# Attention rounds with one weight split each, the next q and k split first, and the sixth sigmoid behind the decoding

## The chip, the cores and the metric

The kernel runs on one core of a Trainium2 chip. Its engines work side by side, each through its own instructions in their order: TensorE (PE, with its weight loads as PEld), VectorE (DVE), ScalarE (ACT), GpSimd (POOL) and SyncE (SP), whose queue issues nearly all DMAs. The metric is the device time of one execution in microseconds (us); of several executions the median counts.

## The reference

Two parts follow each other. The first is an attention with a sigmoid in place of the softmax, for 8 batches, 12 heads, 448 positions and a head size of 64:

```python
scores = scale * np.matmul(q, k.transpose(0, 1, 3, 2)) - np.log(S)
attn = 1.0 / (1.0 + np.exp(-scores))
out = np.matmul(attn, v)
```

The second takes the heads of a position together as x (3584 x 768) and computes a maxout layer with weights of 768 x 768:

```python
h = np.maximum(np.maximum(x @ w1, x @ w2), x @ w3)
return h @ w_out
```

q, k and v come as float32, the weights as 64-bit floats, which the kernel receives as pairs of integers.

## The kernel before, in words

**Precision by splitting.** Most matrix products are made from three products of parts: a tensor is cast to a reduced format (hi) and the remainder is kept (lo), and hi·hi, hi·lo and lo·hi are summed. A split is therefore a cast and a subtraction. For q and k `qk_split` makes it on VectorE (lines 321 and 322, on 128x896 elements); for the weights `w_split` makes it (lines 156 and 157, on 128x384), in the attention on VectorE too.

**The attention in rounds.** `attention` runs 24 rounds (`for n in range(count)`, n from 0 to 23). A round handles four heads, as two pairs; each pair's q and k lie in one tile of 448 KB (`load_qk`, line 302). The 448 keys are three chunks of 128 and one of 64. In a round TensorE does, in this order:

- the scores of the round's second pair, chunks 0 to 2 (line 330, 18 matmuls), read out by `shared_scores`: VectorE copies one head's half (line 385), ScalarE takes the sigmoid of the other (line 387);
- the scores of the next round's first pair, chunks 0 to 2 (line 330, 18 more), each read out by one sigmoid on ScalarE over both heads (line 312). These are called first scores here;
- the products with v (line 350, 24 matmuls);
- the scores of the short fourth chunk for the next round (line 342) and their sigmoid (line 312), and the product of the present round's fourth chunk (line 359).

The score tiles have three buffers in PSUM (`ps_s`), taken in turn. So the first scores of chunk 0 reuse the tile of the second pair's chunk 0, and wait until line 385 and line 387 have read it.

Between the three large sigmoids of the first scores ScalarE also takes the sigmoid of the halves that VectorE copied (`raw_sigmoid`, line 396): large, half, large, half, large, half. The sixth sigmoid of the change's title is the third large one, which goes behind the decoding.

**Work laid beside the rounds.** In each round VectorE and ScalarE also decode one block of the weights (`decode`): ScalarE by lines 178 and 179, VectorE by lines 180, 184, 188 and 189, where line 188 needs line 179. There are three weights q, and for each eight blocks: four that are used first (rounds 0 to 3, 8 to 11, 16 to 19), after the second to fourth of which GpSimd forms sums of blocks (line 144), and four that go back to DRAM (rounds 4 to 7, 12 to 15, 20 to 23) by a DMA that SyncE issues at line 207 and that waits for line 189. Each weight gives seven splits. Before the change `split_weights` makes up to two a round as soon as a weight's four blocks are decoded: rounds 4 to 7, 12 to 15 and 20 to 23 hold 2, 2, 2 and 1. From round 9 on, a slice of the attention's own output is loaded again in each round (line 221, 224 KB), for twelve rounds, and GpSimd forms differences of such slices (line 232).

**The orders.** All of it is pinned in program order on each engine. VectorE's order in a round is: copy out a result of the round before (line 377), three copies of line 385, line 377 again, the split of the next round's second pair, the weight splits, the decoding, and the split of the first pair of the round after that (lines 321 and 322 again). SyncE's order is: load v of the next round (line 307), load the two q and k tiles of the round after that (line 302, twice), store two results (line 378), load a raw weight block (line 168), store the decoded block (line 207, in the rounds named above), load the slice (line 221, in twelve rounds).

The buffers of hi and lo are two of each, so the split of the later first pair overwrites what the present round's first scores read.

After the rounds come four stages of matrix products (line 469), on the same tiles; the first of them needs the splits of x (lines 263 and 267).

Of the kernel before, what the change touches and what calls it, by code (L numbers as in the profile page):

```python
# [27 lines left out]
PRODUCTS = (  # L28
    ("a11", "b11", 0),
    ("s2", "t2", 1),  # L30
    ("s3", "t3", 3),
    ("s1", "t1", 2),
    ("a12", "b21", 0),
    ("a22", "t4", 1),
    ("s4", "b22", 2),
)
# [3 lines left out]
def attention_then_maxout(  # L40
# [35 lines left out]
    C = S // P  # L76
# [50 lines left out]
    def w_stage():  # L127
        return {name: ws_p.tile([P, HP], F32, name=f"ws_{name}") for name in BLOCKS}

    W_ORDER = (("a21", ()), ("a22", ("s1",)), ("a11", ("s2", "s3")), ("a12", ("s4",)))
    W_SUMS = {
        "s1": ("a21", "a22", ALU.add),
        "s2": ("s1", "a11", ALU.subtract),
# [4 lines left out]
    def w_combine(r, names):  # L140
        for name in names:
            r[name] = r["a21"] if name == "s3" else ws_p.tile([P, HP], F32, name=f"ws_{name}")
            in0, in1, op = W_SUMS[name]
            pin(nc.gpsimd.tensor_tensor(out=r[name], in0=r[in0], in1=r[in1], op=op))  # L144

    def w_load(st, q):
        r = w_stage()
        for name, sums in W_ORDER:
            pin(nc.sync.dma_start(out=r[name], in_=w_dram[st, q][:, BLOCKS.index(name)]))
        for name, sums in W_ORDER:  # L150
            w_combine(r, sums)
        return r

    def w_split(q, name, r, copy):
        hi, lo = w_tiles(q, name)
        pin(copy(out=hi, in_=r[name]))
        pin(nc.vector.tensor_tensor(out=lo, in0=r[name], in1=hi.bitcast(F32), op=ALU.subtract))

    def decoding(dec_p, todo, bufs, ahead, square_p):
# [11 lines left out]
        def decode(raw, out):  # L171

            words = raw.bitcast(U32).rearrange("p a (c two) -> p (a c) two", two=2)
            low, high = words[:, :, 0], words[:, :, 1]
            square = square_p.tile([P, S], F32, name="c")[:, :HP]
            bits = dec_p.tile([P, HP], U32, name="wb", bufs=bufs)
            out = bits.bitcast(F32) if out is None else out
            pin(nc.scalar.activation(out=square, in_=high.bitcast(F32), func=AF.Square))  # L178
            pin(nc.scalar.activation(out=low, in_=low, func=AF.Copy, scale=2.0**-29))
            pin(nc.vector.tensor_scalar(  # L180
                out=bits, in0=high, scalar1=3, scalar2=0x3FFFFFF8,
                op0=ALU.logical_shift_left, op1=ALU.bitwise_and,
            ))
            pin(nc.vector.scalar_tensor_tensor(
                out=bits, in0=high, scalar=0xC0000000, in1=bits,
                op0=ALU.bitwise_and, op1=ALU.bitwise_or,
            ))
            pin(nc.vector.tensor_tensor(out=bits, in0=bits, in1=low, op=ALU.add))
            pin(nc.vector.scalar_tensor_tensor(
                out=out, in0=square, scalar=LEAST**2, in1=bits.bitcast(F32),  # L190
                op0=ALU.is_ge, op1=ALU.mult,
            ))
            return out

        for k, (st, q, n) in enumerate(todo):
# [4 lines left out]
            if st == 0:  # L200
                if n == BLOCKS.index(W_ORDER[0][0]):
                    stage = w_stage()
                decode(raws[k], stage[BLOCKS[n]])
                w_combine(stage, dict(W_ORDER)[BLOCKS[n]])
                yield q, stage
# [65 lines left out]
    def attention(stack):  # L271
# [12 lines left out]
        for q in range(3):  # L284
            todo += [(0, q, BLOCKS.index(name)) for name, _ in W_ORDER]
            todo += [(1, q, n) for n in range(4)]
        background = decoding(dec_p, todo, 2, 3, sq_p)
        splits = []

        def decode():  # L290
            done = next(background)
            if done:
                q, stage = done
                decoded.append(q)
                if decoded.count(q) == len(BLOCKS):
                    splits.extend((q, name, stage) for name, _, _ in PRODUCTS)

        decoded = []

# [5 lines left out]
        def load_v(b, f):  # L305
            t = v_p.tile([P, 14, D], F32, name="v")
            pin(nc.sync.dma_start(out=t, in_=v[b, f]))
            return t

        def sigmoid(ps):  # L310
            a = a_p.tile([P, 2, S], F32, name="a")
            pin(nc.scalar.activation(  # L312
                out=a, in_=ps[:, :, :S], func=AF.Sigmoid, bias=bias_s, scale=scale
            ))
            return a[:, 0], a[:, 1]

        def qk_split(t):

            hi = hl_p.tile([P, 2 * S], F32R, name="hi")
            lo = hl_p.tile([P, 2 * S], F32R, name="lo")  # L320
            pin(nc.vector.tensor_copy(out=hi, in_=t))
            pin(nc.vector.tensor_tensor(out=lo, in0=t, in1=hi.bitcast(F32), op=ALU.subtract))
            return (hi, hi), (hi, lo), (lo, hi)

        def scores(terms, c):
            ps = ps_s.tile([P, 2, 512], F32, name="ps_s")
            for n, (kt, qt) in enumerate(terms):
                for e in range(2):
                    r = slice(e * D, (e + 1) * D)
                    pin(nc.tensor.matmul(  # L330
                        ps[:, e, :S], kt[r, S + c * P : S + (c + 1) * P], qt[r, :S],
                        start=n == 0, stop=n == len(terms) - 1,
                    ))
            return ps
# [31 lines left out]
        def load(n):  # L366
            b, f = fours[n]
            return load_qk(b, 2 * f), load_qk(b, 2 * f + 1)

        def finish(n, pss, pool=m_p, names=("m11", "m12"), gs=range(2)):  # L370
            if n < 0:
                return
            b, f = fours[n]
            for g in gs:
                k = 2 * f + g
                o = pool.tile([P, S], F32, name=names[g])
                pin(nc.vector.tensor_copy(out=o, in_=pss[g][:, :S]))
                pin(nc.sync.dma_start(
                    out=x_dram[k // HALF][:, k % HALF, b * S : (b + 1) * S], in_=o
                ))  # L380
# [14 lines left out]
        def raw_sigmoid(a):  # L395
            pin(nc.scalar.activation(
                out=a[1], in_=a[1], func=AF.Sigmoid, bias=bias_s, scale=scale
            ))

        def split_weights():  # L400
            for _ in range(2):
                if splits:
                    w_split(*splits.pop(0), nc.vector.tensor_copy)

        xs, count, pss = {}, len(fours), None
# [6 lines left out]
        for n in range(count):  # L412
            ahead = n + 1 < count
            if ahead:
                next_vt = load_v(*fours[n + 1])
                later_ts = load(n + 2) if n + 2 < count else None
            if n == 0:
                first_terms = qk_split(next_ts[0])
            finish(n - 1, pss, gs=(0,))
            second = [shared_scores(scores(second_terms, c), c) for c in range(C)]  # L420
            finish(n - 1, pss, gs=(1,))
            if ahead:
                second_terms = qk_split(next_ts[1])
            next_first = []
            for c in range(C):
                if ahead:
                    next_first.append(sigmoid(scores(first_terms, c)))
                raw_sigmoid(second[c])
            split_weights()
            decode()  # L430
            if n + 2 < count:
                first_terms = qk_split(later_ts[0])

            part = n - 9
            if 0 <= part < 4 * HALF:
                k, block = divmod(part, 4)
                row, th = ((0, 1), (0, 0), (1, 1), (1, 0))[block]
                x_block(xs, x_dram, 0, row, th, k)
                x_combine(xs, ((), ("t1",), ("t2", "t3"), ("t4",))[block], (k,))
            if n == count - 1:  # L440
                t_store(xs, 0)
                for name in FIRST:
                    x_lo(*x_hi(name, xs))
            pss = [ps_av.tile([P, 512], F32, name=f"ps_av{g}") for g in range(2)]
            for g, weights in enumerate((first, second)):
                for c in range(C):
                    weigh(pss[g], vt, g, c, weights[c])
            next_last = sigmoid(last_scores(next_ts)) if ahead else None
            last_weigh(pss, vt, last)
            if ahead:  # L450
                vt, first, next_ts, last = next_vt, next_first, later_ts, next_last
# [3 lines left out]
    with ExitStack() as stack:  # L455
        xs, finish = attention(stack)
# [196 lines left out]
```

## Time and profile before

| | us |
|---|---|
| median of 3 runs | 873.5 (873.43 to 874.3) |
| the profiled execution, its own time | 874.69 |
| its span in the trace | 872.6 |
| TensorE busy | 858.6 |
| VectorE busy | 661.8 |
| ScalarE busy | 412.5 |
| GpSimd busy | 183.4 |

The profile is of one execution. The span is the time from the first to the last instruction in the trace; the rest of the profiled execution's own time, 2.1 us, lies around it. Busy times are sums over instructions without their waits. In a line of the timeline stand the start, the duration, the engine, the kernel's line, the operation, what it writes and reads, and, in brackets, the idle time of the engine before it and what ended it. A wait is listed as the waiting engine and line, then what it waited for, the total, the times and the longest. The granted TensorE clock is 1.00 throughout.

### The profile page before, as it was taken

The numbers are of one execution on the slowest core, as the hardware profiler recorded it, in microseconds if no ns is written. First come the engines' busy times: TensorE is split into PE (matmuls) and PEld (weight loads), VectorE is DVE, ScalarE is ACT, GpSimd is POOL, SyncE is SP. The second block draws the span as 40 slices with busy tenths as digits, with TensorE's granted clock in tenths as the row PEclk, the third lists the DMA queues.
The fourth block names the chain that finished last, engine by engine and source line by source line (L and its number), as shares of the span: only waits on it lengthen the run. The fifth ranks groups of instructions, "written<-read, shape, count | busy, mean of one in ns | idle before, by whom it ended". The sixth has DMA issues, their size and how long they took to land. (4 is left out here: it accounts for less than half of the span.)

```text
span 872.6 us, 13085 instructions
## 1 busy us (share of the span) xinstructions
PE 858.6 (98%) x4842; PEld 698.7 (80%) x4842; DVE 661.8 (76%) x947; ACT 412.5 (47%) x571; POOL 183.4 (21%) x148
## 2 busy tenths in 40 slices
PE   8999999999999999999999999999999999999998
PEld 4555555555549999999999999999999998999997
DVE  5789878997887868589596888969688798737452
ACT  6778877787783404242352434225344352413320
POOL 0100022012200762702100020210002463760600
PEclk9999999999999999999999999999999999999999
DMA  6667676776638465513836552484653416262422
GB/s 229 207 216 243 225 236 223 251 260 244 216 123 311 164 232 173 191 50 114 324 113 259 196 195 70 131 305 143 235 220 148 169 58 221 90 211 95 170 74 84
DMA packets 74479, 161.88 MB, mean 186 GB/s; under 512 B 6960, under 2 KB 53936, under 8 KB 74416
## 3 DMA queue, kind: packets, MB, share of 16 engines
q1 hardware_dynamic: 74272, 160.94, 52.4%
q8 instruction: 38, 0.62, 0.3%
q14 instruction: 25, 0.20, 0.1%
q10 hardware_dynamic: 144, 0.11, 0.0%
HBM read 109.90 MB, written 51.12 MB: 185 GB/s over the span
## 5 line engine op out<-in xcount | busy, mean ns | idle before, releaser
L469 PE MATMUL ps_y<-xhi_t,wlo_s 128*128 128x448 f32 x432 | 156.8, 363 | 0.0
L469 PE MATMUL ps_y<-xhi_t,whi_s 128*128 128x448 f32 x432 | 156.6, 362 | 0.0
L469 PE MATMUL ps_y<-xlo_t,whi_s 128*128 128x448 f32 x432 | 155.5, 360 | 0.0
L312 ACT ACTIVATE a<-ps_s,bias_s 128x896 f32<-128x896 f32 x96 | 96.5, 1005 | 46.6 <-PE ps_s L342 33.4
L469 PE MATMUL ps_y<-xhi_b,wlo_a 128*128 128x448 f32 x288 | 104.7, 363 | 0.0
L469 PE MATMUL ps_y<-xhi_b,whi_a 128*128 128x448 f32 x288 | 104.4, 362 | 0.0
L469 PE MATMUL ps_y<-xlo_b,whi_a 128*128 128x448 f32 x288 | 103.8, 360 | 0.2 <-DVE xlo_b L267 0.2
L579 ACT COPY p<-ps_y 128x448 f32<-128x448 f32 x48 | 25.5, 531 | 157.6 <-PE ps_y L469 157.5
L144 POOL TENSOR_TENSOR ws_s<-ws_a,ws_a 128x384 f32<-128x384 f32 x12 | 13.4, 1116 | 408.4 <-DMA ws_a<-w_dram 309.9
L469 PEld LDWEIGHTS ps_y<-xhi_t,whi_s 128*128 128x128 f32 x432 | 81.1, 188 | 6.5
L469 PEld LDWEIGHTS ps_y<-xlo_t,whi_s 128*128 128x128 f32 x432 | 80.8, 187 | 5.6
L469 PEld LDWEIGHTS ps_y<-xhi_t,wlo_s 128*128 128x128 f32 x432 | 81.1, 188 | 4.2
L553 DVE TENSOR_TENSOR m<-ps_y,u 128x448 f32<-128x448 f32 x71 | 43.8, 620 | 50.8 <-PE ps_y L469 49.3
L582 DVE TENSOR_TENSOR u<-ps_y,p 128x448 f32<-128x448 f32 x48 | 29.8, 622 | 53.9 <-PE ps_y L469 49.9
L232 POOL TENSOR_TENSOR xs_t<-xs_b,xs_t 128x448 f32<-128x448 f32 x48 | 63.1, 1341 | 36.0 <-DMA xs_b<-x_dram 35.8
L551 ACT COPY m<-ps_y 128x448 f32<-128x448 f32 x24 | 12.8, 533 | 121.0 <-PE ps_y L469 114.2
L267 DVE TENSOR_TENSOR xlo_t<-xs_t,xhi_t 128x1344 fp32r<-128x1344 f32 x42 | 67.8, 1614 | 0.0
L267 DVE TENSOR_TENSOR xlo_b<-xs_b,xhi_b 128x1344 fp32r<-128x1344 f32 x42 | 67.2, 1599 | 0.1
L330 PE MATMUL ps_s<-hi 64*128 64x448 f32 x282 | 57.8, 395 | 5.4 <-DVE half L385 5.2
L178 ACT ACTIVATE c<-wraw 128x384 f32<-128x384 f32 x48 | 26.7, 556 | 74.6 <-DVE m L559 43.6
L263 ACT CAST xhi_t<-xs_t 128x1344 fp32r<-128x1344 f32 x42 | 55.4, 1318 | 12.2 <-PE ps_y L469 8.0
L263 ACT CAST xhi_b<-xs_b 128x1344 fp32r<-128x1344 f32 x42 | 55.4, 1318 | 9.6 <-PE ps_y L469 9.6
(71 smaller groups left out, 1820.5 us busy)
## 6 DMA issues: line engine op xcount, KB each, us to landing
qk<-qk SPq DMA_DIRECT2D x48, 448.0 KB, 5.5
xs_b<-x_dram SPq DMA_DIRECT2D x30, 672.0 KB, 6.6
wraw<-w SPq DMA_DIRECT2D x36, 384.0 KB, 5.7
xs_t<-t_dram SPq DMA_DIRECT2D x18, 672.0 KB, 7.9
v<-v SPq DMA_DIRECT2D x24, 448.0 KB, 3.4
h_dram<-m SPq DMA_DIRECT2D x48, 224.0 KB, 1.9
xs_b<-h_dram SPq DMA_DIRECT2D x16, 672.0 KB, 6.2
outT<-m SPq DMA_DIRECT2D x47, 224.0 KB, 1.9
```

Of the source, the lines that this page charges most:

```text
L144: pin(nc.gpsimd.tensor_tensor(out=r[name], in0=r[in0], in1=r[in1], op=op))
L178: pin(nc.scalar.activation(out=square, in_=high.bitcast(F32), func=AF.Square))
L232: pin(nc.gpsimd.tensor_tensor(out=r[name][:, k], in0=r[in0][:, k], in1=r[in1][:, k], op=ALU.subtract))
L263: pin(nc.scalar.copy(out=hi, in_=r[name]))
L267: pin(nc.vector.tensor_tensor(out=lo, in0=x, in1=hi.bitcast(F32), op=ALU.subtract))
L312: pin(nc.scalar.activation(out=a, in_=ps[:, :, :S], func=AF.Sigmoid, bias=bias_s, scale=scale))
L330: pin(nc.tensor.matmul(ps[:, e, :S], kt[r, S + c * P : S + (c + 1) * P], qt[r, :S], start=n == 0, stop=n == len(terms) - 1,))
L469: pin(nc.tensor.matmul(ps[:, :S], wt[:, k * P : (k + 1) * P], xt[:, k], start=first and n == 0, stop=n == len(terms) - 1, skip_group_check ...
L551: pin(nc.scalar.copy(out=m[name], in_=y))
L553: pin(nc.vector.tensor_tensor(out=m[name], in0=y, in1=add, op=ALU.add))
L579: pin(nc.scalar.copy(out=p1, in_=ps[0][:, :S]))
L582: pin(nc.vector.tensor_tensor(out=u2, in0=ps[1][:, :S], in1=p1, op=ALU.add))
```

## The change

Four things change in `attention`.

- The order in which a weight's seven splits are queued is a list of its own, W_SPLITS, instead of the order of the products.
- `split_weights` makes one split a round up to round 20, and two in rounds 21 to 23. With the splits becoming available in rounds 4, 12 and 20, rounds 4 to 10, 12 to 18 and 20 hold one, rounds 21, 22 and 23 two.
- On VectorE the split of the later first pair comes directly behind the split of the next second pair, ahead of the weight split and the decoding.
- On ScalarE the third large sigmoid of the first scores comes behind the last half's sigmoid and the two decoding instructions. TensorE's order stays.

SyncE's order stays as well.

```diff
+    W_SPLITS = ("s3", "a22", "s1", "a11", "s2", "a12", "s4")
...
-                    splits.extend((q, name, stage) for name, _, _ in PRODUCTS)
+                    splits.extend((q, name, stage) for name in W_SPLITS)
...
-        def split_weights():
-            for _ in range(2):
+        def split_weights(most):
+            for _ in range(most):
                 if splits:
                     w_split(*splits.pop(0), nc.vector.tensor_copy)
...
             if ahead:
                 second_terms = qk_split(next_ts[1])
             next_first = []
-            for c in range(C):
+            for c in range(C - 1):
                 if ahead:
                     next_first.append(sigmoid(scores(first_terms, c)))
                 raw_sigmoid(second[c])
-            split_weights()
-            decode()
+            raw_sigmoid(second[C - 1])
+            last_ps = scores(first_terms, C - 1) if ahead else None
             if n + 2 < count:
                 first_terms = qk_split(later_ts[0])
+            split_weights(1 if n + 3 < count else 2)
+            decode()
+            if ahead:
+                next_first.append(sigmoid(last_ps))
```

## The prediction

> **What bounds the kernel now.** I read the page first, then the waits, then the timeline of the attention, round by round.
>
> ```profile
> PE 858.6 (98%) x4842; PEld 698.7 (80%) x4842; DVE 661.8 (76%) x947; ACT 412.5 (47%) x571; POOL 183.4 (21%) x148
> ```
>
> TensorE is busy for 98% of the span, which seems to leave no room. It doesn't settle the matter for the attention, where the same matmuls take rounds of different length. Each row below is the first score matmul of a round: rounds 0, 12, 18, 20 and 23 (I call these times T0, T12 and so on).
>
> ```profile
> 9.85 0.47 PE L330 MATMUL ps_s<-hi 64*128 64x448 f32 x2
> ...
> 137.38 0.47 PE L330 MATMUL ps_s<-hi 64*128 64x448 f32 x2
> ...
> 200.32 0.47 PE L330 MATMUL ps_s<-hi 64*128 64x448 f32 x2
> ...
> 222.39 0.47 PE L330 MATMUL ps_s<-hi 64*128 64x448 f32 x2
> ...
> 254.19 0.47 PE L330 MATMUL ps_s<-hi 64*128 64x448 f32 x2
> ```
>
> Rounds 18 and 19 take 11.03 us each (22.07 by 2). Round 13, from the rows of its two ends, takes 10.36:
>
> ```profile
> 148.38 0.47 PE L330 MATMUL ps_s<-hi 64*128 64x448 f32 x2
> ...
> 158.74 0.47 PE L330 MATMUL ps_s<-hi 64*128 64x448 f32 x2
> ```
>
> The waits name the difference (the third row is of SP's queue):
>
> ```profile
> PE ps_s L330 <- DVE half L385: 5.2, 9, 0.6
> ...
> DVE wb L188 <- ACT wraw L179: 33.9, 22, 2.9
> ```
>
> ```profile
> SPq L207 <- DVE wb L189: 194.1, 36, 12.8
> ```
>
> Nine times TensorE waits, recorded at 0.6, for VectorE's copy of line 385; and VectorE itself waits in most rounds for ScalarE's line 179. So the limit is a ring: line 179, then VectorE's lines 188, 189, 321, 322, 377, 385, then the first scores, their sigmoids, and line 179 again. The nine are the rounds after a GpSimd sum:
>
> ```profile
> 125.62 1.25 POOL L144 TENSOR_TENSOR ws_s<-ws_s,ws_a 128x384 f32<-128x384 f32 x1 [9.77 <-DVE ws_a L189]
> 126.05 1.78 DVE L322 TENSOR_TENSOR lo<-qk,hi 128x896 fp32r<-128x896 f32 x1
> ...
> 127.74 0.61 DVE L377 COPY m<-ps_av 128x448 f32<-128x448 f32 x1
> 128.28 0.61 DVE L385 COPY half<-ps_s 128x448 f32<-128x448 f32 x1
> ```
>
> ```profile
> 129.03 0.47 PE L330 MATMUL ps_s<-hi 64*128 64x448 f32 x2 [0.59 <-DVE half L385]
> ```
>
> Line 322 takes 1.78 us beside GpSimd and 1.09 elsewhere (below, at 158.65), 0.69 more: the whole of 11.03 less about 10.34. The first scores start 1.29 after line 377.
>
> Even the short rounds carry a little of the ring. In round 13 pairs of matmuls follow each other by 0.20, but the first scores start 0.30 after the pair before them, and their second pair 0.27 later:
>
> ```profile
> 149.90 0.36 PE L330 MATMUL ps_s<-lo,hi 64*128 64x448 f32 x2
> 150.10 0.37 PE L330 MATMUL ps_s<-hi,lo 64*128 64x448 f32 x2
> 150.40 0.47 PE L330 MATMUL ps_s<-hi 64*128 64x448 f32 x2
> 150.67 0.39 PE L330 MATMUL ps_s<-lo,hi 64*128 64x448 f32 x2
> ```
>
> Without the wait that is 0.10 and 0.06 or so less: a floor of 10.36 - 0.16 = 10.20 us a round, with first scores at T+1.92 (150.30 less 148.38).
>
> **The sixth sigmoid (ScalarE).** It leaves the path to line 179:
>
> ```profile
> 154.22 1.00 ACT L312 ACTIVATE a<-ps_s,bias_s 128x896 f32<-128x896 f32 x1
> 155.11 0.67 ACT L396 ACTIVATE half<-half,bias_s 128x448 f32<-128x448 f32 x1
> ```
>
> Lines 178 and 179 come 0.89 us earlier (155.11 - 154.22). The sigmoid itself then ends about a microsecond behind line 179, still ahead of the fourth chunk's scores, and its PSUM tile is wanted only by the next round's chunk 1: cost nothing, covered by ScalarE's idle time (47% busy).
>
> **VectorE's order.** The rows of one round's end and SP's rows between them:
>
> ```profile
> 148.92 0.90 SPq L302 DMA_DIRECT2D qk<-qk  x2
> ...
> 154.99 0.35 DVE L156 CAST whi_s<-ws_s 128x384 fp32r<-128x384 f32 x1
> ...
> 155.85 0.35 DVE L180 TENSOR_SCALAR wb<-wraw 128x384 uint32<-128x384 uint32 x1
> ...
> 158.00 0.62 DVE L321 CAST hi<-qk 128x896 fp32r<-128x896 f32 x1
> 158.11 0.32 SPq L207 DMA_DIRECT2D w_dram<-wb  x1
> ...
> 158.65 1.09 DVE L322 TENSOR_TENSOR lo<-qk,hi 128x896 fp32r<-128x896 f32 x1
> ...
> 159.46 0.90 SPq L302 DMA_DIRECT2D qk<-qk  x2
> 159.66 0.62 DVE L377 COPY m<-ps_av 128x448 f32<-128x448 f32 x1
> ```
>
> One weight split is 0.86 (154.99 to 155.85), the decoding 2.15 (155.85 to 158.00), a q and k split 1.66 (158.00 to 159.66); line 207 goes out 0.11 after VectorE has finished decoding. Where VectorE is not late, as in the last round, it is through with its copies at T+3.23 (257.42 less 254.19):
>
> ```profile
> 257.42 0.35 DVE L156 CAST whi_s<-ws_s 128x384 fp32r<-128x384 f32 x1
> ...
> 259.63 0.56 DVE L188 CUSTOM_DVE_ANT_0 wb<-wraw,wb 128x768 uint16<-128x768 uint16 x1 [0.40 <-ACT wraw L179]
> ```
>
> New order: second pair split to T+4.89, first pair split to 6.55, one weight split to 7.41, decoding to 9.56. To leave TensorE alone, line 377 must start by 1.92 - 1.29 = 0.63 of the next round, T+10.83. So there are 1.27 us to spare, the ring through line 179 is broken, and GpSimd's sums now run beside line 377 and copies out of PSUM, not beside line 322. Line 232's differences may still meet a q and k split; one such meeting, at the 0.69 above, is covered by the 1.27. That is the gain: each round falls to 10.20.
>
> **What is late next.** The first pair's split now stands ahead of everything, and it waits for its tile, loaded in the same round. The load is issued at T+0.54 (148.92 - 148.38). Queued behind the waiting line 321 are the weight split, the decoding, and in SP's queue, behind line 207's wait for line 189, the slice, the next v and the next q and k. Landing times of the first of the two loads, asked for alone, in rounds 2, 6, 13, 14, 15, 16 and 21:
>
> ```profile
> DMA to landing us min/median/max: 4.0/4.0/4.0
> ```
>
> ```profile
> DMA to landing us min/median/max: 4.9/4.9/4.9
> ```
>
> ```profile
> DMA to landing us min/median/max: 5.2/5.2/5.2
> ```
>
> ```profile
> DMA to landing us min/median/max: 5.9/5.9/5.9
> ```
>
> ```profile
> DMA to landing us min/median/max: 6.3/6.3/6.3
> ```
>
> ```profile
> DMA to landing us min/median/max: 5.4/5.4/5.4
> ```
>
> ```profile
> DMA to landing us min/median/max: 6.7/6.7/6.7
> ```
>
> Round 6 stands for ordinary rounds: landing at T+5.44, VectorE done at 5.44 + 1.66 + 0.86 + 2.15 = 10.11, before 10.83. No loss, 0.7 to spare.
>
> Rounds 12 to 15 and 20 both store a block (line 207) and load a slice behind it. There a second ring closes: line 207 to the q and k issue 1.35 (158.11 to 159.46), the landing, and from the landing back to line 207 4.67 + 0.11 = 4.78. With 5.2, 5.9, 6.3 and 5.4 this makes 11.33, 12.03, 12.43 and 11.53 a turn, all above 10.20. From T12 on: line 207 of round 12 at 5.44 + 4.78 = 10.22; four loads with their 1.35 take 28.20, three returns 14.34, the last 4.67: VectorE is done with round 16 at T12+57.43, the first scores of round 17 start at 58.72, and T18 follows at 58.72 + 8.28 = 67.00. Before, T12 to T18 was 62.94.
> In the same way from T20: 10.22 + 1.35 + 6.7 + 4.67 + 0.86 (round 21 holds two splits) = 23.80, first scores of round 22 at 25.09, T23 at 33.37; before, 31.80.
>
> **Last round.** One split more, 0.86, less the 0.40 that line 188 waits now: the splits of x start 0.46 later, and TensorE already waits for them:
>
> ```profile
> 262.44 0.47 PE L469 MATMUL ps_y<-xlo_b,whi_a 128*128 128x448 f32 x1 [0.18 <-DVE xlo_b L267]
> ```
>
> **The sum**, against the profiled 874.69: T0 to T12 goes from 127.53 to 122.40, -5.13; T12 to T18 +4.06; T18 to T20 from 22.07 to 20.40, -1.67; T20 to T23 +1.57; the end +0.46. Together -0.71, about 874.0; on the median of 873.5, which lies 1.2 below the profiled run, 872.8. The stages after it are TensorE's own and only shift. The list W_SPLITS costs nothing by itself: each staged block is split at least a round before the next weight overwrites it.
>
> **Unknown: the landing under the new order.** No row shows these loads when line 207 itself is late. Between the nearest rows, 4.9 and 6.7, I take each round's own, as the traffic is the same.
>
> **Rivals.** (1) With a late line 207 the earlier transfers of the round are through, and the loads land as in round 6, in 4.9. Turns of 11.03: T18 at 63.80 and T23 at 31.57, so -5.13 + 0.86 - 1.67 - 0.23 + 0.46 = -5.7, 867.8. For it: round 13 needed only 5.2. Against: 5.9 and 6.3 came with nothing else left over from the round before.
> (2) The loads land fast enough that no turn exceeds 10.20, that is within 10.20 - 4.78 - 1.35 = 4.07 us. All 23 rounds at the floor: 234.60 instead of 244.34, with the end -9.3, 864.2. Round 2's 4.0 is that short, but there neither a store of line 207 nor a slice goes ahead; of the five loads with both ahead the shortest is 5.2.
> [...]
> (3) Slower: the second ring turns at the slowest row, 6.7, in all four links: 4 more us (26.8 for 22.8), +3.3, 876.8. It decides from a mean landing of 5.9 (no gain) and is slower by more than can be doubted from 6.3. For it: the landing grew with every round in a row, 5.2, 5.9, 6.3.
> (4) The floor isn't reached: the 0.16 belongs to the change of operands, not to the ring. The 16 rounds outside the second ring keep it, 16 x 0.16 = 2.6: +1.9, 875.4. Against: changes of chunk show no such gap.
>
> **How the numbers follow.** Forecast 0.46, rivals 0.20, 0.06, 0.16 and 0.12. About 0.2% (1.75 us) can be told from no change. The forecast's own range is 0.3 us a landing either way, 871.3 to 874.3: 0.12 of it faster, 0.31 same, 0.03 slower. Rivals 1 and 2 give 0.25 faster and 0.01 same; rival 3 0.13 slower and 0.03 same; rival 4 half and half. Faster 0.37, same 0.41, slower 0.22. The range 867.5 to 876 takes in rival 1, rival 4 and half of rival 3.
>
> **What would show it.** Right: no wait of TensorE for line 385 in rounds 2 to 4, 10 to 12 and 18 to 20, the first six of them rounds at 10.2; no line 322 of 1.78; line 188's wait nearly gone; a wait of line 321 for its DMA in most rounds; rounds 14 to 17 and 22 at 11 to 12.5. Wrong: rounds 14 to 17 at 10.2 (rivals 1, 2), ordinary rounds still at 10.35 (rival 4), or line 321 holding up rounds 5 to 8 as well.

## The result and the profile after

The changed kernel takes 880.04 us in the median of six executions (877.24 to 884.21), the kernel before 873.99; the ratio is 1.0074 with a 95% interval of 1.0049 to 1.0100. It is slower, outside the predicted range of 867.5 to 876, and it varies by 7 us where the kernel before varies by 1. The profiled execution is the shortest of the six, 877.24 (span 875.2), so its trace shows the lower end of the cost: 2.55 more than the profiled execution before.

The lines named so far have moved by two: 322 is now 324, 385 is 387, 207 is 209, and so on. The waits of the changed kernel in the attention (waiting engine and line, then what it waited for: us in total, times, longest):

```profile
DVE hi L323 <- DMA qk<-qk: 28.7, 15, 4.4
...
PE ps_s L332 <- DVE half L387: 9.6, 8, 2.7
```

VectorE's wait for line 181 (33.9 us before) is no longer listed. In its place VectorE waits 28.7 us for the q and k tile, up to 4.4 at once, and TensorE's wait for VectorE's copy has grown from 5.2 us in nine pieces of at most 0.6 to 9.6 in eight of up to 2.7. The starts of rounds 0, 12, 18, 20 and 23:

```profile
9.59 0.47 PE L332 MATMUL ps_s<-hi 64*128 64x448 f32 x2
...
133.77 0.47 PE L332 MATMUL ps_s<-hi 64*128 64x448 f32 x2
...
204.12 0.47 PE L332 MATMUL ps_s<-hi 64*128 64x448 f32 x2
...
224.45 0.47 PE L332 MATMUL ps_s<-hi 64*128 64x448 f32 x2
...
256.99 0.47 PE L332 MATMUL ps_s<-hi 64*128 64x448 f32 x2
```

| stretch | before | predicted | after |
|---|---|---|---|
| T0 to T12 | 127.53 | 122.40 | 124.18 |
| T12 to T18 | 62.94 | 67.00 | 70.35 |
| T18 to T20 | 22.07 | 20.40 | 20.33 |
| T20 to T23 | 31.80 | 33.37 | 32.54 |
| T0 to T23 | 244.34 | 243.17 | 247.40 |

All of the loss is in the attention: from T23 to the end both spans have the same length, 618.4 (872.6 less 254.19) and 618.2 (875.2 less 256.99). Rounds 12 to 17 take 7.4 us more than before and rounds 20 to 22 0.7 more; the other rounds gain 5.1.

One turn of the second ring, in SyncE's queue, on VectorE and then on TensorE:

```profile
155.71 0.32 SPq L209 DMA_DIRECT2D w_dram<-wb  x1
156.09 0.42 SPq L223 DMA_DIRECT2D xs_b<-x_dram  x1
156.60 0.41 SPq L309 DMA_DIRECT2D v<-v  x1
157.06 0.42 SPq L304 DMA_DIRECT2D qk<-qk  x1
```

```profile
155.13 0.56 DVE L191 SCALAR_TENSOR_TENSOR wb<-c,wb 128x384 f32<-128x384 f32 x1
...
164.02 0.63 DVE L323 CAST hi<-qk 128x896 fp32r<-128x896 f32 x1 [4.02 <-DMA qk<-qk]
...
168.71 0.62 DVE L379 COPY m<-ps_av 128x448 f32<-128x448 f32 x1
```

```profile
170.00 0.47 PE L332 MATMUL ps_s<-hi 64*128 64x448 f32 x2 [2.67 <-DVE half L387]
```

Line 191 ends at 155.69, the store goes out at 155.71, and the q and k load, third behind it, at 157.06: 1.35 later, as in the sum. It lands at 164.0, where line 323 starts after 4.02 us of idling. Line 379 of the next round starts 4.69 after that, and TensorE, whose next round began at 165.24, gets its first scores at 170.00, 2.8 us late.

### The profile page after: what moved, and what is told of

It reads as the page before. It is cut to its first block, busy times and chain, and to the rows that moved or that the text cites. A ratio compares the mean times of both kernels' runs of the same rounds, so it can differ in the third digit from the quotient of the medians.

```text
span 875.2 us, 13084 instructions
## 1 busy us (share of the span) xinstructions
PE 857.1 (98%) x4842; PEld 699.5 (80%) x4842; DVE 660.0 (75%) x947; ACT 411.5 (47%) x571; POOL 177.0 (20%) x148
## 5 line engine op out<-in xcount | busy, mean ns | idle before, releaser
L332 PE MATMUL ps_s<-hi 64*128 64x448 f32 x282 | 56.0, 389 | 9.6 <-DVE half L387 9.6
```

What stands on the lines that cost most here:

```text
L332: pin(nc.tensor.matmul(ps[:, e, :S], kt[r, S + c * P : S + (c + 1) * P], qt[r, :S], start=n == 0, stop=n == len(terms) - 1,))
```

## The experiments

Theory A: the time goes into the second ring (load, first pair's split, weight split, decoding, store, and behind the store in SyncE's queue the next load). Theory B: the moved sigmoid or the spread weight splits cost it. Theory C: a tile that is loaded in the round of its split lands too late for a split that stands ahead, whatever the queue's order.

### The split put back

```diff
-            if n + 2 < count:
-                first_terms = qk_split(later_ts[0])
             split_weights(1 if n + 3 < count else 2)
             decode()
+            if n + 2 < count:
+                first_terms = qk_split(later_ts[0])
```

> The changed kernel with the later first pair's split put back behind the decoding; the sixth sigmoid and the one weight split a round stay. Theory A (a second ring: q and k load, first pair's split, weight split, decoding, store of the decoded block, and behind that store in SyncE's queue the next load): no wait for the load is left, VectorE is free at about T+10.3, rounds of 10.2 us nearly throughout, rounds behind a GpSimd sum 10.2 to 10.4: 865 us (863 to 867). Theory B (the moved sigmoid or the spread weight splits cost the time): 878 or more, as the changed kernel.

Measured: 865.09 us, ratio to before 0.9897 (0.9884 to 0.9911). Rounds 0 and 23 start so:

```profile
10.04 0.47 PE L332 MATMUL ps_s<-hi 64*128 64x448 f32 x2
...
244.29 0.47 PE L332 MATMUL ps_s<-hi 64*128 64x448 f32 x2
```

That is 234.25 for 23 rounds, 10.18 each. Theory B falls: with the sigmoid moved and the splits spread the kernel is 9 us faster than before; it is the place of the q and k split that costs, 15 us between this kernel and the changed one. GpSimd still holds VectorE up (line 324 takes 1.77 us instead of 1.09), as here behind round 1's sum, and it does no harm:

```profile
28.70 1.31 POOL L146 TENSOR_TENSOR ws_s<-ws_a,ws_a 128x384 f32<-128x384 f32 x1 [28.26 <-DVE ws_a L191]
29.19 1.77 DVE L324 TENSOR_TENSOR lo<-qk,hi 128x896 fp32r<-128x896 f32 x1
```

### The sigmoid alone

```diff
-            for c in range(C):
+            for c in range(C - 1):
...
+            raw_sigmoid(second[C - 1])
+            last_ps = scores(first_terms, C - 1) if ahead else None
             split_weights()
             decode()
+            if ahead:
+                next_first.append(sigmoid(last_ps))
```

> The kernel before with the sixth sigmoid moved behind the decoding and nothing else. Theory A: the gain of the change is the sigmoid's 0.89 us on the first ring; VectorE with two weight splits is free at T+10.4, under 10.83: 865 us (863 to 867), rounds of 10.2. Theory B: 874 or more. A third, that the gain of the ordinary rounds came from the split that went ahead and not from the sigmoid: 873 to 875.

Measured: 864.33 us, ratio 0.9888 (0.9873 to 0.9903), the fastest of all. 234.62 from T0 to T23:

```profile
9.07 0.47 PE L330 MATMUL ps_s<-hi 64*128 64x448 f32 x2
...
243.69 0.47 PE L330 MATMUL ps_s<-hi 64*128 64x448 f32 x2
```

The gain of the change is the sigmoid, whole: 0.89 us off the first ring is enough for every round but the first to come to TensorE's floor (10.17 to 10.23), two weight splits and GpSimd's sums included.

### The split ahead alone

```diff
+            if n + 2 < count:
+                first_terms = qk_split(later_ts[0])
             split_weights()
             decode()
-            if n + 2 < count:
-                first_terms = qk_split(later_ts[0])
```

> The kernel before with the later first pair's split put ahead of the weight splits and the decoding, and nothing else: two splits in rounds 4 to 6, 12 to 14 and 20 to 22, the sigmoid in its old place. Theory A: a turn of the second ring gets 0.86 longer than in the changed kernel in the rounds of two splits, rounds 6 to 8 become slow as well, and rounds 13 to 15 and 21, 22 more so: 884 us (879 to 890). Theory B: 865 to 874, since neither the sigmoid nor the splits have moved.

Measured: 880.86 us, ratio 1.0080 (1.0064 to 1.0096), within the expected 879 to 890. T12 to T18 takes 69.64:

```profile
135.80 0.47 PE L330 MATMUL ps_s<-hi 64*128 64x448 f32 x2
...
205.44 0.47 PE L330 MATMUL ps_s<-hi 64*128 64x448 f32 x2
```

Two turns of the second ring, from store to store, hold a second weight split and take 12.92 and 13.39, against 12.23 and 13.10 in the changed kernel. The stretch as a whole isn't longer than the changed kernel's 70.35: round 16 holds no weight split here, and the four landings are 1.6 us shorter together. Rounds 1 to 4 run at 10.17 with the sigmoid in its old place, so the split ahead breaks the first ring as well.

### One weight split a round alone

```diff
-        def split_weights():
-            for _ in range(2):
+        def split_weights(most):
+            for _ in range(most):
...
-            split_weights()
+            split_weights(1 if n + 3 < count else 2)
```

with the new list W_SPLITS.

> The kernel before with the weight splits spread (one a round, two in the last three) in the new order, and nothing else. Theory A: VectorE waits for line 179 in every round anyway, so rounds of two splits are not the limit: 874 us, plus up to 0.5 for the second split in the last round (873.5 to 875). If the spread splits carry a part of the gain or loss: under 872 or over 876.

Measured: 875.15 us, ratio 1.0014 (1.0005 to 1.0024): next to nothing, 0.15 above the expected range. T0 to T23 is 244.5, as before, so the spread splits carry no part of the attention's gain or loss. Whether the second split of the last round makes the 1.2 us isn't shown: without T0 to T23 the span is 629.4 us here and 628.2 before, but this rest also differs between the other runs (627.1 with the sigmoid alone, 628.9 with the split put back).

### The store behind the loads

```diff
-                pin(nc.sync.dma_start(out=w_dram[st, q][:, n], in_=decode(raws[k], None)))
+                bits = decode(raws[k], None)
...
+                    held.append((w_dram[st, q][:, n], bits))
...
                 later_ts = load(n + 2) if n + 2 < count else None
+            for out, bits in held:
+                pin(nc.sync.dma_start(out=out, in_=bits))
+            held.clear()
...
+        for out, bits in held:
+            pin(nc.sync.dma_start(out=out, in_=bits))
```

The last two lines stand behind the rounds, for the block of the last round.

> The changed kernel, but SyncE issues the store of a decoded block behind the next round's loads of v, q and k instead of ahead of them, so no load waits for the decoding any more. Theory A: the second ring is open, loads land 4.5 to 6.5 after an issue at T+0.54, VectorE is done by 10.1 to 11.5: rounds 14 to 17 at 10.2 to 10.8, 865 us (864 to 869). Rival C (the tile simply lands too late for a split that stands ahead, whatever the order of the queue, by the traffic of these rounds): rounds 14 to 17 stay above 11, 875 or more.

Measured: 872.43 us, ratio 0.9977 (0.9967 to 0.9988), which lies between the two forecasts. The trace tells them apart: T12 to T18 takes 61.16, six rounds at 10.19, as theory A has it (lines 330, 469 and 263 are 337, 485 and 269 in this kernel).

```profile
133.20 0.47 PE L337 MATMUL ps_s<-hi 64*128 64x448 f32 x2
...
194.36 0.47 PE L337 MATMUL ps_s<-hi 64*128 64x448 f32 x2
```

The time is lost behind the attention. The last block's store was left to the very end, behind the stores of the x differences, and a later tile that takes its memory waited for it; first the matmul, then the wait of ScalarE's cast:

```profile
261.17 0.47 PE L485 MATMUL ps_y<-xhi_t,wlo_s 128*128 128x448 f32 x1 [3.59 <-ACT xhi_t L269]
```

```profile
ACT xhi_t L269 <- DMA w_dram<-wb: 6.6, 1, 6.6
```

So the kernel was mended: the last round's store goes out at once.

```diff
+            if n == count - 1:
+                for out, bits in held:
+                    pin(nc.sync.dma_start(out=out, in_=bits))
             part = n - 9
```

> As the run before with the stores behind the next loads, but in the last round the store goes out at once, ahead of the stores of the x differences, so that no later tile waits for it. Theory A (the second ring closes through SyncE's queue): attention rounds at 10.17 as in that run, and no wait of 3.6 us at the start of the products: 865 us (864 to 867). If the loss after the attention has another cause than that last store: 872 again.

Measured: 866.18 us, ratio 0.9909 (0.9892 to 0.9925), and T12 to T18 is 61.00:

```profile
132.86 0.47 PE L337 MATMUL ps_s<-hi 64*128 64x448 f32 x2
...
193.86 0.47 PE L337 MATMUL ps_s<-hi 64*128 64x448 f32 x2
```

Every part of the change is still in this kernel; only SyncE's order differs. The loads of rounds 13 to 16 are issued at T+0.54 again and land in 4.5 to 4.8 us, that of round 14 so:

```profile
DMA to landing us min/median/max: 4.5/4.5/4.5
```

Theory C falls, and the loss, 14 us between the changed kernel and this one, is shown to run through the queue. With the other order the loads are issued earlier and also take less time (4.5 to 4.8 us instead of 6.0 to 6.9); this run doesn't separate the two.

### q and k ahead of v

```diff
-                next_vt = load_v(*fours[n + 1])
                 later_ts = load(n + 2) if n + 2 < count else None
+                next_vt = load_v(*fours[n + 1])
```

> The changed kernel with the loads of q and k issued ahead of the load of v. Theory A: the ring stays, but a turn gets shorter by the issue and the transfer of v, 0.4 + 1.4 us; turns in rounds 13 to 16 of about 10.3 instead of 11.8, ordinary rounds clear: 868 us (865 to 871). If the ring were not what limits rounds 14 to 17 and the split's place alone were: no change, 878 to 882.

Measured: 865.97 us, ratio 0.9914 (0.9899 to 0.9929), a little better than expected (the 1.4 us for the transfer of v was the author's estimate). The ring is still closed, but the first loads of rounds 13 to 16 land in 4.0 to 4.3 us instead of 6.0 to 6.9; that of round 14:

```profile
DMA to landing us min/median/max: 4.1/4.1/4.1
```

With 0.89 from the store to the issue (v's issue no longer lies between) and 4.89 from the landing to the next store, a turn is about 0.89 + 4.1 + 4.89 = 9.9 (from round 13's store to round 14's it is 9.92), under the floor of 10.17, and rounds 13 to 16 run at 10.17 (round 17 still at 10.82). It is a matter of size, as a ring should be: the turn of 9.9, under TensorE's round, cost nothing, and the changed kernel's, 12.23 and 13.10 among them, lie over it, where T12 to T18 took 70.35 instead of six times 10.17.

### Stalls made on purpose

TensorE ran some of the changed kernel's first scores at a granted clock of 0.50 (0.37 us a pair in round 16 instead of 0.20), which no theory had. What such a wait costs was measured by itself on the kernel before, with VectorE's first copy of line 385 repeated.

```diff
+        def shared_scores(ps, c, more=0):
...
-            copy = nc.vector.tensor_copy(out=a[1], in_=ps[:, 1, :S])
-            pin(copy)
+            copies = []
+            for _ in range(1 + more):
+                copies.append(nc.vector.tensor_copy(out=a[1], in_=ps[:, 1, :S]))
+                pin(copies[-1])
...
+            more = 4 if n in (5, 6, 7, 8) else 0
+            second = [shared_scores(scores(second_terms, c), c, more * (c == 0)) for c in range(C)]
```

> The kernel before with VectorE's first copy of a round made five times instead of once in rounds 5 to 8, which holds the first scores up by about 2.1 us in each. If TensorE's clock is left alone by waits of 2 us: 874 + 8.5 = 882.5 us, all score matmuls at 0.20, clock 1.0. If waits of this size already lower the clock: 884 or more and pairs at 0.37.

Measured: 885.62 us, ratio 1.0137 (1.0122 to 1.0152). The waits came out at 2.55 (2.26 in round 8) instead of 2.1, so the time alone doesn't decide; the pairs do. In three of the four rounds the scores behind them run at 0.20 a pair; in round 7, behind this wait, they run at 0.37 (line 385 is 387 in this kernel):

```profile
93.67 0.74 PE L330 MATMUL ps_s<-hi 64*128 64x448 f32 x2 [2.55 <-DVE half L387]
```

```profile
94.00:96.00 2.00, 2.00 (x12) 1.93 (x12) 1.97 (x5) 0.80 (x1) 0.00 (x0) 0.50 0.65 254
```

(In this view by stretches the third number from the right is the granted clock.) With ten copies in rounds 5 and 13:

> The kernel before with VectorE's first copy made ten times in rounds 5 and 13, which holds the first scores up by about 5 us in each. Without an effect on the clock 2 x 5.2: 884.5 us. With half the clock behind a wait of that length in both rounds, 1.4 us or more each on top: 887 to 889, first scores at 0.37 a pair in both rounds.

Measured: 890.15 us in two executions, ratio 1.0184 (1.0154 to 1.0213), a little above the expected range, as the waits came out longer. In both rounds the granted clock falls to 0.50; the first:

```profile
71.99 0.74 PE L330 MATMUL ps_s<-hi 64*128 64x448 f32 x2 [5.84 <-DVE half L387]
```

```profile
70.00:72.00 2.00, 0.01 (x2) 0.04 (x2) 1.93 (x4) 0.00 (x0) 0.00 (x0) 0.50 0.12 45
72.00:74.00 2.00, 2.00 (x11) 1.93 (x13) 1.97 (x4) 0.48 (x1) 0.00 (x0) 0.50 0.00 0
```

The first scores of rounds 5 and 13 take 3.12 from the first pair to the last, where 1.70 is usual: 1.4 us on top of each wait.

### The changed kernel again

> The changed kernel once more, to see which rounds differ between executions: the first profile was of an execution of 877.2, the median is 880.0. Theory A with TensorE's clock: rounds 14 to 17 and 22 again at 11 to 15 us, and where an execution is longer, turns of the second ring with later landings, or first scores at 0.37 a pair behind a long wait, make the difference; everything outside those rounds the same within 1 us. If the difference lies after the attention, theory A lacks a part.

> The changed kernel a third time, for the same comparison: by theory A the attention's length from T0 to T23 explains the time of each execution within 1 us, whatever it is; between 246 and 254 us for executions of 876 to 884.

Measured: 877.22 us (874.09 to 882.89), ratio 1.0041 (1.0017 to 1.0064), and 877.83 (874.54 to 881.46), ratio 1.0048 (1.0029 to 1.0068): slower again, less than in the first set. The profiled executions took 874.09 and 874.54, the first of them with

```profile
9.29 0.47 PE L332 MATMUL ps_s<-hi 64*128 64x448 f32 x2
...
253.89 0.47 PE L332 MATMUL ps_s<-hi 64*128 64x448 f32 x2
```

so 244.60 from T0 to T23, the second with 243.84. With the first profile (247.40 at 877.24) the attention's length explains the execution's time to within 1.2 us, a little worse than the 1 us expected: the rests are 629.8, 629.5 and 630.7. In the three profiles no rounds but 2, 7 to 9, 14 to 17 and 22 are longer than 10.3. But each profiled execution is the shortest of its set; the long ones, up to 884, were not traced. Most of them have a lower mean granted clock, down to 0.992 at 881.46 us, which would fit more stretches at 0.50. In which rounds these lie, and whether they cost time or only go with longer waits, was not seen.

## Why the prediction was wrong

**What held.** The first ring, that the change breaks it, and the floor: rounds without a wait take 10.17 (predicted 10.20). The second ring too is there as described, and both ways out of it, through the queue's order and through the landing time, worked. The end cost nothing visible (predicted 0.46).

**What failed: the size of the second ring.** The prediction weighed a gain of 9.3 us against a loss of 8.6 in the second ring, and sized that loss by the landings ("I take each round's own, as the traffic is the same": 5.2, 5.9, 6.3, 5.4 and 6.7). The same loads of the changed kernel, in rounds 13, 14, 15, 16 and 21:

```profile
DMA to landing us min/median/max: 6.0/6.0/6.0
...
DMA to landing us min/median/max: 6.9/6.9/6.9
...
DMA to landing us min/median/max: 6.1/6.1/6.1
...
DMA to landing us min/median/max: 6.3/6.3/6.3
...
DMA to landing us min/median/max: 5.6/5.6/5.6
```

Above the floor of 10.17 the first profile loses 9.3 in rounds 12 to 17, 2.0 in rounds 20 to 22 and 2.2 in rounds that the prediction had clear (2 and 7 to 9): 13.5 instead of 8.6. The stretch T12 to T18, term by term, in the three profiles of the changed kernel:

| | predicted | first | second | third |
|---|---|---|---|---|
| T12 to the store of round 12 | 10.22 | 9.71 | 9.71 | 10.42 |
| four landings | 22.80 | 25.33 | 23.83 | 22.90 |
| four times from store to load, three from landing to store | 19.74 | 20.06 | 20.09 | 20.07 |
| last landing to the first scores of round 17 | 5.96 | 6.91 | 6.88 | 6.89 |
| from there to T18 | 8.28 | 8.34 | 8.34 | 8.37 |
| T12 to T18 | 67.00 | 70.35 | 68.85 | 68.66 |

In the first profile the landings are most of the miss, 2.5 us; in the third they are as short as predicted, and the stretch is still 1.7 too long. What all three have is the fourth row, 0.9 more than the sum had:

```profile
192.76 1.40 POOL L234 TENSOR_TENSOR xs_t<-xs_b,xs_t 128x448 f32<-128x448 f32 x1 [5.18 <-DMA xs_b<-x_dram]
```

```profile
193.18 1.40 DVE L191 SCALAR_TENSOR_TENSOR ws_a<-c,wb 128x384 f32<-128x384 f32 x1
194.50 0.61 DVE L379 COPY m<-ps_av 128x448 f32<-128x448 f32 x1
```

Beside a difference on GpSimd line 191 takes 1.40 instead of 0.56 (1.37 and 1.38 in the other two profiles). The prediction had such a meeting, with a q and k split, called it "covered by the 1.27" and gave it nothing. That holds only where VectorE has 1.27 to spare; in a round in which it is late already, the 0.84 is paid in full. The other 0.1 of this row and the third row's 0.3 are the 0.09 from each landing to line 323, and rounding.

In rounds 20 to 22 the error went the other way: the load of round 21 landed in 5.6 instead of 6.7, and the stretch is 0.8 shorter than predicted.

**What was called free and wasn't: ordinary rounds.** "No loss, 0.7 to spare": rounds 7 and 8 take 10.79 and 10.78.

```profile
81.46 0.47 PE L332 MATMUL ps_s<-hi 64*128 64x448 f32 x2
...
92.25 0.47 PE L332 MATMUL ps_s<-hi 64*128 64x448 f32 x2
...
103.03 0.47 PE L332 MATMUL ps_s<-hi 64*128 64x448 f32 x2
```

Rounds 5 to 8 too have a store in the round before them (without a slice), so the second ring is closed there as well; the sum followed it only where a slice lies in it. From store to load it is 0.84 there, and with landings of 5.1 to 5.4 and the 4.89 back to the store a turn takes 10.8 to 11.1, above the floor. The issue of round 5's load is at T+0.54, of round 6's at 1.15, of round 7's at 2.08, and the 0.7 is used up in three rounds. Rounds 7 to 9 lose 1.46, and round 2 another 0.70 behind a load of 6.9 us. That makes T0 to T12 1.8 longer than predicted. Line 321 holding up rounds 5 to 8 was among the prediction's own signs of being wrong.

**What was not in the sum and cost nothing in these profiles: the clock.** In round 16 the scores behind the wait start every 0.37 instead of 0.20:

```profile
182.37 0.49 PE L332 MATMUL ps_s<-hi 64*128 64x448 f32 x2 [1.92 <-DVE half L387]
...
183.34 0.64 PE L332 MATMUL ps_s<-hi 64*128 64x448 f32 x2
183.71 0.64 PE L332 MATMUL ps_s<-lo,hi 64*128 64x448 f32 x2
```

The granted clock is 0.50 there, and round 17 starts 9.87 after these first scores, where round 16 started 8.35 after those of round 15: 1.5 later. But TensorE waits in round 17 all the same:

```profile
195.78 0.47 PE L332 MATMUL ps_s<-hi 64*128 64x448 f32 x2 [1.45 <-DVE half L387]
```

The load that VectorE works on was issued at 182.53, before the clock fell (at 182.69), and from its landing at 188.9 to line 379 at 194.50 VectorE doesn't wait for TensorE. So without the half clock this wait would only have been longer. In the third profile the same holds for round 15 (2.78 from the first pair to the last): the first scores of round 16 are still late there, 2.21 after its start instead of 1.93. A slow stretch cost nothing where another engine was later still; behind the ten copies, where VectorE was not late in the next round, it cost 1.4 us each.

**What stays open.** The miss is 7.2 us of the median (880.04 against 872.8), and the profile locates 3.2 of it (877.24 against 874.0): 1.8 + 3.35 - 0.8 - 0.1 in the attention, less 1.0 behind it. The other 4.0 lies between executions: the median of the six is 2.8 above the profiled one, and the prediction had taken off 1.2 because the profiled execution before lay above its median. The second ring passes each late landing on to the round, so a spread is to be expected, but the runs don't show which rounds make the long executions long.

Of the rivals, the faster ones were wrong. Rival 3's 876.8 is near the first profile's 877.24, but partly by luck: the mean landing of 6.7 that it took came in none of the three profiles (6.3, 6.0 and 5.7), and the rest was made up by terms that it didn't have. The measured single edits don't add up to the change (-9.7, +6.8 and +1.2): the sigmoid and the split ahead break the same first ring, so its gain is to be had once, and the sigmoid alone has it without the second.

## What to carry to other kernels

When work is moved ahead of a wait for a load, follow the waiting engine's later work into the queue that issues the loads: if a store there waits for that work, the next load stands behind it, and the loads can become a ring that is late in every round. Follow it in every round where such a store stands, compare the length of one turn with the round, and where the turn is longer, count each landing's spread and each meeting with another engine in full: nothing there is covered by spare time. And try the parts alone: here one of three edits held the whole gain.

## What the runs showed of the hardware

In these runs a wait of TensorE could cost more than its length. Behind a recorded wait of 5.84 us the granted clock was 0.50 and nine score pairs took 1.4 us more, in both rounds; behind waits of 2.55 it was so in one round of three; in the changed kernel behind one of 1.92, but not behind one of 2.67 in the round before.

In the changed kernel's first profile the stretch at 0.50 is 3.41 us long; in each row the number behind the stretch's length is TensorE's busy time, and the third from the right the clock:

```profile
179.28:182.69 3.41, 1.49 (x16) 1.10 (x14) 3.21 (x7) 1.85 (x3) 0.00 (x0) 1.00 0.17 62
182.69:186.10 3.41, 3.41 (x20) 2.83 (x18) 2.75 (x5) 2.46 (x4) 1.11 (x1) 0.50 0.92 260
186.10:189.52 3.42, 3.42 (x20) 1.26 (x18) 0.55 (x1) 2.90 (x5) 1.48 (x2) 1.00 0.95 318
```

The one behind the wait of 2.55 is about as long (mean clocks of 0.85, 0.50 and 0.80 in three stretches of 2 us make 3.4 at 0.50), the first one with ten copies about twice as long (0.78 over 4 us, 0.50 over 4 and 0.72 over 2 make 6.9).

What decides whether the clock falls behind a wait isn't shown. TensorE's busy time just before doesn't tell the changed kernel's two waits apart: in the 3.41 us before the first scores that ended the wait of 2.67 it was 0.74, before those that ended the wait of 1.92 it was 1.49, and the clock fell behind the second only:

```profile
166.59:170.00 3.41, 0.74 (x8) 0.38 (x5) 3.20 (x8) 1.47 (x3) 0.00 (x0) 1.00 0.10 40
178.96:182.37 3.41, 1.49 (x18) 1.07 (x14) 3.20 (x8) 1.85 (x3) 0.00 (x0) 1.00 0.12 45
```
